# Laying out a pair's queries half a step later, between two value products that share one PSUM buffer

## The chip, the cores and the metric

The kernel runs on one core of a Trainium2 chip. The metric is the device time of one execution in microseconds, the median of several runs. Engines are named as in the profile: PE is TensorE's matmul row and PEld its weight loads, DVE is VectorE, ACT is ScalarE, POOL is GpSimd, SP issues DMAs.

## What is computed

Sliding-window attention with a few sink keys, then a dense MLP over its output, then a mixture of experts. In the reference, cut to what matters:

```python
scores = scale * np.matmul(q, k.transpose(0, 1, 3, 2))       # 4 x 8 heads, 768 x 768, head size 64
keep = is_sink | in_window                                   # 4 sink keys, window of 128
scores = np.where(keep, scores, -1000000000.0)
a = softmax(scores)
x = np.matmul(a, v)                                          # becomes 3072 tokens x 512
h = np.maximum(x @ w_in, 0.0)                                # 512 -> 2048
x = h * h @ w_out                                            # 2048 -> 512
# then: gate logits, one expert of 8 per token, two more products, scaled
```

## The kernel before

The work has three stages: a start in which weights are converted and split into a high and a low part, a first MLP with the attention laid into it (to about 820 us), and the experts. The change concerns the second.

The 3072 tokens are taken in 12 blocks of 256. A pass of the first MLP goes over one block: 16 hidden products (`l1`, L546, twelve matmuls of 256 columns, because each operand is split in two) and 16 output products (`l2`, L562, six matmuls of 512 columns) two steps behind. Each hidden or output product is a half-step, so a pass has 32 of them. `l1`'s result is squared and split on ScalarE and VectorE (L549, L550, L552, L553).

While pass t - 1 runs, the attention of block t is computed, cut into events that carry a time in half-steps. `attn_events` lists them and `run_to` emits those that are due after each half-step. A block has 8 heads in four pairs p of two heads, and two query tiles n of 128 for each pair. The events are:

- `prep_k`: the keys of a pair are transposed on TensorE (L319) and copied and split.
- `prep_q`: the queries of a pair are transposed (L345, two matmuls with the identity) into a PSUM tile `psq`; ScalarE copies the high part (L356), VectorE subtracts for the low part (L357). The values of the pair are split on GpSimd (L363, L364), and `more` issues the loads of the pair after the next.
- `scores`: the score products (L404), mask and maximum on VectorE (L408, L410), exponential on ScalarE (L412), the sum's reciprocal (L414, L415), scaling on ScalarE (L424), and the sink part on GpSimd (L427 to L429).
- `ptrans`: the weights are transposed (L439), copied and split (L450 or L458, L451 or L459), and masked on GpSimd (L455).
- `pv`: the value products (L479) into a PSUM tile `pso`, read by ScalarE (L484 to L486) and VectorE (L487, L488).
- `fin_sink` and `add_sink` at the end of a block: the sink weights are transposed (L496) and multiplied with the sink values (L504) into a PSUM tile `pso2`, read by VectorE (L505).

`psq`, `pso` and `pso2` have the same tag in the pool `psO`, which has one buffer:

```python
psO = ps1.enter_context(tc.tile_pool(name="psO", bufs=1, space=PSUM))
ps = psO.tile([128, 4, 128], F32, tag="O", name="psq")
ps = psO.tile([128, 2, 2, 128], F32, tag="O", name="pso")
```

The times of the events come from the table `LEADS`, with one row for block 0, one for block 1 and one for all later blocks (columns: lead of `prep_k`, lead of `prep_q`, lag of `ptrans`, lag of `pv`):

```python
h0 = 32 * (t - 1) - 8
a0, a1, a2, a3 = LEADS[min(t, 2)]
ev.append((h0 + 8 * p - a1, lambda p=p: prep_q(t, p)))
ev.append((h0 + 4 * n + a3, lambda n=n: pv(t, n // 2, n % 2)))
```

The gate of the block before runs in the same pass, in four pieces (`gate_pieces`): two with four transposes each (L592; ScalarE L601 and L603, VectorE L602, GpSimd L604), the logits (L615, a chain of small VectorE operations and two exponentials on ScalarE, L633 and L634), and the places (L649, L650). They meet pair 2, pair 3, pair 0 and pair 1 in this order, eight half-steps apart. At the end of a pass `split_x` splits the attention's output into the input of the next pass (L512 on ScalarE, L513 on VectorE).

The code is written in the order of these events, and a scheduler then sets the order of each engine's queue from it; each engine executes its queue in that order.

Of the kernel before, what the change touches and what calls it, by code (L numbers as in the profile page):

```python
# [31 lines left out]
T32 = 2  # L32


LEADS = ((5, 2, 4.5, 8.5), (5, 2, 4.5, 8), (5.5, 2.5, 4.5, 8))

SPLITS = {6: (0, 0), 8: (2, 0), 11: (0, 1), 12: (1, 0), 13: (2, 1), 14: (3, 0)}
NSLOT = NT // 128 + NE - 1
# [4 lines left out]
def kern(ctx, tc, q, k, v, n_sink, window, w_in, w_out, w_gate, w_og, w1, w2, out):  # L43
# [471 lines left out]
    def attn_events(t):  # L515

        ev = []
        h0 = 32 * (t - 1) - 8
        a0, a1, a2, a3 = LEADS[min(t, 2)]
        for p in range(4):  # L520
# [578 lines left out]
```

## Time and profile before

| what | value |
|---|---|
| median of 3 runs | 1193.41 us (1192.56 to 1198.88) |
| the profiled execution, its own time | 1196.3 us |
| its span, first to last instruction | 1194.5 us |
| busy in the span: PE, PEld | 1138.7 us (95%), 945.7 us (79%) |
| busy in the span: DVE, ACT, POOL | 761.5, 626.5, 457.9 us |
| L546 (hidden products), matmuls | 314.8 us, 2304 of 285 ns |
| L562 (output products), matmuls | 159.0 + 157.8 us, 1152 of 410 ns |
| L345 (query transposes), matmuls | 21.7 us, 96 of 305 ns |
| mean granted clock of TensorE | 0.991 of full |

The matmul rows overlap one another, since matmuls are pipelined: the distance between two starts says more than the sum of durations. Times below are counted from the span's start.

### The profile page before, as it was taken

The page shows a single profiled execution, that of the slowest core. Times are in us where ns is not written, and L with a number is a line of the kernel's source. Part 1 is how long each engine was busy: PE and PEld are TensorE (multiplying, and loading weights), DVE is VectorE, ACT ScalarE, POOL GpSimd, SP SyncE. Part 2 cuts the span into 40 slices and gives each one's busy share as a digit, 9 for nine tenths or more (in the row PEclk, how much of TensorE's full clock was granted, in tenths as well). Part 3 has the DMA queues.
Part 4 walks back from the last instruction along what each step waited for, and adds up shares of the span by engine and source line. Part 5 has one row for each costly group of instructions (what it writes and reads, how often), then busy time and mean ns, then how long its engine had stood idle before and what let it go on. Part 6 is the DMA issues. An engine that isn't in the chain of part 4 may idle for free. (4 is left out here: it accounts for less than half of the span.)

```text
span 1194.5 us, 24037 instructions
## 1 busy us (share of the span) xinstructions
PE 1138.7 (95%) x7022; PEld 945.7 (79%) x7022; DVE 761.5 (64%) x2123; ACT 626.5 (52%) x1740; POOL 457.9 (38%) x949
## 2 busy tenths in 40 slices
PE   4898889999999999999999999999899999999996
PEld 2476678888888888888888888887788888888884
DVE  4699776767676667676767677656611466764153
ACT  3677576767666766666676666545222222222200
POOL 4256665326565335555424556310211222222111
PEclk9999899999999999999999999999999999999998
DMA  4565411111211211121112120087411357554110
GB/s 123 132 181 176 137 35 45 32 51 37 54 32 28 50 37 46 35 49 29 47 35 51 37 54 1 19 182 207 133 39 44 100 179 255 189 203 151 42 51 23
DMA packets 139387, 100.08 MB, mean 84 GB/s; under 512 B 103903, under 2 KB 112223, under 8 KB 139234
## 3 DMA queue, kind: packets, MB, share of 16 engines
q1 hardware_dynamic: 132674, 83.85, 25.1%
q0 software_dynamic: 5472, 14.19, 3.6%
q8 instruction: 64, 1.05, 0.4%
q14 instruction: 89, 0.73, 0.3%
q10 hardware_dynamic: 1088, 0.26, 0.1%
HBM read 85.56 MB, written 13.76 MB: 83 GB/s over the span
## 5 line engine op out<-in xcount | busy, mean ns | idle before, releaser
L546 PE MATMUL psh<-xT,WI 128*128 128x256 f32 x2304 | 314.8, 285 | 10.6 <-POOL WI L284 8.1
L546 PEld LDWEIGHTS psh<-xT,WI 128*128 128x128 f32 x2304 | 294.9, 190 | 29.0 <-POOL WI L284 10.9
L867 PE MATMUL psh<-WI,xt 128*128 (+1 forms) x672 | 164.8, 400 | 0.3 <-ACT ht L847 0.3
L562 PE MATMUL psx<-WOb,h 128*128 128x512 f32 x576 | 157.8, 410 | 2.7 <-ACT h L552 2.4
L562 PE MATMUL psx<-WOa,h 128*128 128x512 f32 x576 | 159.0, 409 | 0.0
L867 PEld LDWEIGHTS psh<-WI,xt 128*128 128x128 f32 x672 | 124.3, 188 | 27.9 <-ACT xt L847 0.5
L550 DVE TENSOR_TENSOR r<-r 128x256 f32<-128x256 f32 x184 | 83.6, 455 | 68.3 <-ACT r L549 66.7
L562 PEld LDWEIGHTS psx<-WOb,h 128*128 128x128 f32 x576 | 102.6, 191 | 23.4 <-ACT h L552 3.9
L412 ACT ACTIVATE P<-P,st 128x260 f32<-128x260 f32 (+1 forms) x192 | 92.7, 485 | 47.4 <-DVE st L410 45.1
L883 DVE TENSOR_TENSOR ht<-psht,ht 128x512 fp32r<-128x512 f32 x56 | 38.5, 689 | 123.9 <-ACT ht L847 123.5
L549 ACT ACTIVATE r<-psh 128x256 f32<-128x256 f32 x192 | 72.2, 377 | 83.6 <-PE psh L546 72.4
L562 PEld LDWEIGHTS psx<-WOa,h 128*128 128x128 f32 x576 | 102.1, 190 | 17.4 <-issue 0.3
L553 DVE TENSOR_TENSOR h<-r,h 128x256 fp32r<-128x256 f32 x192 | 91.9, 479 | 29.3 <-ACT h L552 25.7
L905 POOL DMA_INDIRECT out_dram<-xg,pidx x28 | 31.2, 1116 | 193.5 <-ACT xg L904 152.0
L408 DVE CUSTOM_DVE_ANT_0 P<-pss,M 128x260 f32<-128x260 f32 (+1 forms) x184 | 72.5, 403 | 28.2 <-PE pss L404 14.3
L455 POOL TENSOR_SCALAR_AFFINE_SELECT PT<-PT 128x256 fp32r<-128x256 f32 x224 | 85.1, 415 | 12.9 <-DVE st L410 12.8
L552 ACT ACTIVATE h<-r 128x256 fp32r<-128x256 f32 x192 | 78.1, 408 | 22.2 <-DVE r L550 18.0
L896 PE MATMUL psy<-WOb,ht 128*128 (+1 forms) x336 | 85.1, 402 | 0.0
L896 PE MATMUL psy<-WOa,ht 128*128 (+1 forms) x336 | 84.1, 397 | 0.0
L873 ACT ACTIVATE r<-psh 128x512 f32<-128x512 f32 x48 | 28.7, 598 | 99.7 <-PE psh L867 97.8
L838 POOL DMA_INDIRECT xg<-x2tab,pidx x30 | 40.7, 1356 | 95.5 <-issue 55.9
L489 POOL TENSOR_TENSOR xr<-tB,tC 128x128 f32<-128x128 f32 x80 | 37.6, 470 | 97.8 <-DVE tB L488 95.3
(430 smaller groups left out, 1979.3 us busy)
## 6 DMA issues: line engine op xcount, KB each, us to landing
raw<-in_moe_w_dram SPq DMA_DIRECT2D x36, 1024.0 KB, 6.2
craw<-in_moe_w_in_dram SPq DMA_DIRECT2D x16, 512.0 KB, 3.8
craw<-in_moe_w_out_dram SPq DMA_DIRECT2D x16, 512.0 KB, 3.2
x2tab<-x2s SPq DMA_DIRECT2D x24, 256.5 KB, 3.1
kn<-in_k_dram SPq DMA_DIRECT2D x64, 96.0 KB, 2.3
vn<-in_v_dram SPq DMA_DIRECT2D x64, 96.0 KB, 2.2
qn<-in_q_dram SPq DMA_DIRECT2D x92, 64.0 KB, 2.1
kn<-in_k_dram SPq DMA_DIRECT2D x32, 64.0 KB, 2.1
```

What stands on the lines that cost most here:

```text
L408: V.tensor_tensor_reduce(out=P[:, e, 0:W], in0=ps[e][:, 0:W], in1=mask[:, 0:W], scale=1.0, scalar=-3.0e38, op0=ALU.add, op1=ALU.max, accum ...
L412: A.activation(out=P[:, e, 0:W], in_=P[:, e, 0:W], func=AF.Exp, scale=SCALE, bias=st[:, 2 + e:3 + e], accum_out=st[:, 4 + e:5 + e])
L455: G.affine_select(out=both[:, 1 - b, e], in_=bf[:, 0, e], pattern=[[0, 2], [1 - 2 * b, 128]], compare_op=ALU.is_gt if b else ALU.is_ge, fi ...
L546: PE.matmul(ps[:], lhsT=WI[:, j, a_, kk, :], rhs=x[:, b_, kk, :], start=(n == 0), stop=(n == 11))
L549: A.activation(out=hq[:], in_=ps[:], func=AF.Relu)
L550: (G if t == 0 and j % 2 else V).tensor_tensor(out=hq[:], in0=hq[:], in1=hq[:], op=ALU.mult)
L552: A.activation(out=o[:, 0], in_=hq[:], func=AF.Copy)
L553: V.tensor_tensor(out=o[:, 1], in0=hq[:], in1=o[:, 0].bitcast(F32), op=ALU.subtract)
L562: PE.matmul(acc[t][m][:], lhsT=o[:, a_, 128 * m:128 * m + 128], rhs=WO[j // 8][:, j % 8, b_, :], start=(j == 0 and n == 0), stop=(j == NF ...
L838: G.indirect_dma_start(out=x, out_offset=None, in_=x2tab[:] if s >= PRE else x2tab[0:256 * (NBLK - 3)], in_offset=bass.IndirectOffsetOnAxi ...
L867: PE.matmul(ps[:], lhsT=o[:, a_, kk, :], rhs=wview(n, par + 2048 * b_ + 512 * kk, 512), start=(c == 0), stop=(c == 11))
L896: PE.matmul(yp[s][:], lhsT=o[:, a_, kk, :], rhs=wview(2 + n, par + 2048 * b_ + 512 * kk, 512), start=(n == 0 and kk == 0 and c == 0), stop ...
```

## The change

For the blocks from 2 on, `prep_q` has a lead of 1.5 half-steps where it had 2.5. The value products of the pair before are at 0 and 4 half-steps (of eight), so the layout was emitted after half-step 5 and is now emitted after half-step 6, halfway to the next value product. Ten blocks with four pairs each are touched, 40 of the 48 layouts. No instruction is added or taken away.

```diff
-LEADS = ((5, 2, 4.5, 8.5), (5, 2, 4.5, 8), (5.5, 2.5, 4.5, 8))
+LEADS = ((5, 2, 4.5, 8.5), (5, 2, 4.5, 8), (5.5, 1.5, 4.5, 8))
```

What this does to the queues shows at three places. In the names, `psx` is the output products' accumulator, `psh` a hidden product, `psg` the gate's tile, `pss` scores, `h` the split hidden values.

TensorE, a pair that meets the gate's transposes, before:

```order
L439 MATMUL pspt<-ident,P 128x128 x2
L562 MATMUL psx_7034<-WOa,h_7114 128x512 x3
L562 MATMUL psx_7035<-WOa,h_7114 128x512 x3
L345 MATMUL psq<-ident,qn 128x128 x2
L546 MATMUL psh<-xT,WI 128x256 x12
L592 MATMUL psg<-ident,x2s 128x128 x4
L562 MATMUL psx_7034<-WOa,h_7185 128x512 x3
L562 MATMUL psx_7035<-WOa,h_7185 128x512 x3
L546 MATMUL psh<-xT,WI 128x256 x12
L479 MATMUL pso<-PT,V 128x256 x4
```

Here the query transposes stand right behind the output products, ahead of the hidden one. With the change:

```order
L439 MATMUL pspt<-ident,P 128x128 x2
L562 MATMUL psx_7034<-WOa,h_7114 128x512 x3
L562 MATMUL psx_7035<-WOa,h_7114 128x512 x3
L546 MATMUL psh<-xT,WI 128x256 x12
L592 MATMUL psg<-ident,x2s 128x128 x4
L345 MATMUL psq<-ident,qn 128x128 x2
L562 MATMUL psx_7034<-WOa,h_7185 128x512 x3
L562 MATMUL psx_7035<-WOa,h_7185 128x512 x3
L546 MATMUL psh<-xT,WI 128x256 x12
L479 MATMUL pso<-PT,V 128x256 x4
```

The query transposes moved behind one hidden product and the gate's four transposes; one output and one hidden product remain between them and the value products.

ScalarE at the same place, before:

```order
L450 ACTIVATE PT<-pspt 128x2x128
L356 ACTIVATE qT<-psq 128x256
L412 ACTIVATE P,st<-P,st 128x260 x2
L549 ACTIVATE r<-psh 128x256
L601 ACTIVATE x2T<-psg 128x512
L424 ACTIVATE P<-P,st 128x132 x2
L552 ACTIVATE h_7310<-r 128x256
L603 ACTIVATE x2T<-x2U 128x512
L549 ACTIVATE r<-psh 128x256
L484 ACTIVATE tB<-pso 128x256
```

Here L356 stands ahead of the two exponentials (L412). With the change:

```order
L450 ACTIVATE PT<-pspt 128x2x128
L412 ACTIVATE P,st<-P,st 128x260 x2
L549 ACTIVATE r<-psh 128x256
L601 ACTIVATE x2T<-psg 128x512
L424 ACTIVATE P<-P,st 128x132 x2
L552 ACTIVATE h_7290<-r 128x256
L603 ACTIVATE x2T<-x2U 128x512
L356 ACTIVATE qT<-psq 128x256
L549 ACTIVATE r<-psh 128x256
```

The copy of the query tile (L356) moved from ahead of the exponentials to behind L603, the second copy of the gate's transposes.

TensorE at the end of a pass, a pass in which the sink values are added, before (the query transposes stand ahead of these rows, two groups earlier):

```order
L504 MATMUL pso_7832<-pskT,vsk 128x256 x2
L562 MATMUL psx_7034<-WOb,h_7689 128x512 x3
L562 MATMUL psx_7035<-WOb,h_7689 128x512 x3
L562 MATMUL psx_7034<-WOb,h_7727 128x512
L509 COMPARE_AND_BRANCH
L509 UNCONDITIONAL_BRANCH x2
L562 MATMUL psx_7034<-WOb,h_7727 128x512 x2
L562 MATMUL psx_7035<-WOb,h_7727 128x512 x3
L479 MATMUL pso<-PT,V 128x256 x4
L404 MATMUL pss_7871<-kT,qT 128x260
```

Here the sink products (L504) come after the query tile has been read, and the value products come straight behind the output products. With the change:

```order
L504 MATMUL pso_7812<-pskT,vsk 128x256 x2
L562 MATMUL psx_7034<-WOb,h_7689 128x512 x3
L562 MATMUL psx_7035<-WOb,h_7689 128x512 x3
L562 MATMUL psx_7034<-WOb,h_7727 128x512 x2
L509 COMPARE_AND_BRANCH
L509 UNCONDITIONAL_BRANCH x2
L345 MATMUL psq<-ident,qn 128x128 x2
L562 MATMUL psx_7034<-WOb,h_7727 128x512
L562 MATMUL psx_7035<-WOb,h_7727 128x512 x3
L404 MATMUL pss_7871<-kT,qT 128x260
L404 MATMUL pss_7872<-kT,qT 128x260
L404 MATMUL pss_7871<-kT,qT 128x260
```

The query transposes now stand behind the sink products, with eight output products between. The value products follow the last row, so three of the six score products stand ahead of them.

## Rows read from the trace of the kernel before

**Rows 1.** Busy time by stretches: us; busy PE, PEld, DVE, ACT, POOL; clock, DMA, GB/s.

```profile
350.00:430.00 80.00, 78.45 (x559) 68.04 (x559) 54.56 (x195) 54.53 (x170) 36.70 (x90) 1.00 0.15 35
```

**Rows 2.** Groups by line, the whole run: busy us, mean ns | idle before, releasers.

```profile
L345 PE MATMUL psq<-ident,qn 128*128 128x128 f32 x96 | 21.7, 305 | 6.6 <-ACT PT L450 2.7 <-issue 0.9 <-DVE qT L352 0.5
...
L345 PEld LDWEIGHTS psq<-ident,qn 128*128 128x128 f32 x96 | 10.8, 148 | 23.7 <-issue 18.3 <-ACT PT L450 4.5 <-DVE qT L352 0.8
```

**Rows 3.** Waits of PE from 200 to 1000 us: us in total, times, longest.

```profile
PE psq L345 <- ACT PT L450: 2.7, 3, 1.0
...
PE psst L496 <- POOL psk L429: 1.1, 3, 0.5
```

**Rows 4.** Timeline of PE, a pair at the gate's transposes: start us, duration us.

```profile
364.59 0.64 PE L479 MATMUL pso<-PT,V 128*128 128x256 f32 x4
...
365.92 1.64 PE L562 MATMUL psx<-WOa,h 128*128 128x512 f32 x6
...
367.69 0.41 PE L345 MATMUL psq<-ident,qn 128*128 128x128 f32 x2
...
367.85 1.65 PE L546 MATMUL psh<-xT,WI 128*128 128x256 f32 x12
...
369.34 0.60 PE L592 MATMUL psg<-ident,x2s 128*128 128x128 f32 x4
...
369.69 1.64 PE L562 MATMUL psx<-WOa,h 128*128 128x512 f32 x6
...
371.17 1.57 PE L546 MATMUL psh<-xT,WI 128*128 128x256 f32 x12
...
372.58 0.64 PE L479 MATMUL pso<-PT,V 128*128 128x256 f32 x4
```

**Rows 5.** Timeline of ACT and DVE in the same stretch.

```profile
367.18 0.29 DVE L488 TENSOR_TENSOR tB<-pso,tB 64x128 f32<-64x128 f32 x1
...
368.13 0.38 ACT L356 ACTIVATE qT<-psq 128x256 fp32r<-128x256 f32 x1 [1.12 <-PE psq L345]
...
368.20 0.16 DVE L410 TENSOR_SCALAR st<-st 128x2 f32<-128x2 f32 x1
...
368.42 0.50 ACT L412 ACTIVATE P<-P,st 128x260 f32<-128x260 f32 x1
...
368.55 0.42 DVE L357 TENSOR_TENSOR qT<-psq,qT 128x256 fp32r<-128x256 f32 x1 [0.20 <-ACT qT L356]
...
368.91 0.50 ACT L412 ACTIVATE P<-P,st 128x260 f32<-128x260 f32 x1
...
369.60 0.38 ACT L549 ACTIVATE r<-psh 128x256 f32<-128x256 f32 x1
...
369.98 0.60 ACT L601 ACTIVATE x2T<-psg 128x512 bf16<-128x512 f32 x1
...
370.18 0.40 DVE L550 TENSOR_TENSOR r<-r 128x256 f32<-128x256 f32 x1
...
370.47 0.69 ACT L424 ACTIVATE P<-P,st 128x132 f32<-128x132 f32 x2
...
370.61 0.69 DVE L602 TENSOR_TENSOR x2U<-psg,x2T 128x512 f32<-128x512 f32 x1
...
371.06 0.41 ACT L552 ACTIVATE h<-r 128x256 fp32r<-128x256 f32 x1
...
371.37 0.62 ACT L603 ACTIVATE x2T<-x2U 128x512 bf16<-128x512 f32 x1
...
371.50 0.42 DVE L553 TENSOR_TENSOR h<-r,h 128x256 fp32r<-128x256 f32 x1 [0.20 <-ACT h L552]
```

**Rows 6.** Timeline at the end of a pass, PE and DVE.

```profile
338.12 0.48 PE L504 MATMUL pso<-pskT,vsk 128*128 128x256 f32 x2
...
339.50 0.68 DVE L505 TENSOR_TENSOR xr<-pso,xr 128x512 f32<-128x512 f32 x1
...
341.24 0.63 PE L479 MATMUL pso<-PT,V 128*128 128x256 f32 x4
```

## The prediction

> **What bounds the kernel now.** I read the busy time by stretches first. In the steady part of the first MLP, with the attention spread through it, TensorE is busy for 78.45 of 80 us at full clock and no other engine is busy for more than 55 [rows 1]. So a change of order gains only what TensorE waits, and it loses whatever new wait it creates on TensorE. Next come the groups by line. The query transposes (L345) are preceded by 6.6 us of idle time on the matmul row over the whole run, and by 23.7 us on the weight-load row [rows 2]. The list of waits then gives the two waits that matter below. Three query transposes waited 2.7 us in all, put down to ScalarE's copy of PT, and three sink transposes waited 1.1 us for GpSimd [rows 3].
>
> The page doesn't name the real releaser, so I went to the timeline. The query transposes and the value products share one PSUM buffer (tag O, one copy). The transposes can start only when VectorE's last read of the earlier value product (L488) is done. L488 ends at 367.18 + 0.29 = 367.47 [rows 5], and the transposes start at 367.69 [rows 4]: 0.22 us from the end of a VectorE read to the start of the matmul that waited for it. In the same rows the output products (L562) start at 365.92 and the transposes 1.77 later. The next six output products, with nothing that waits behind them, need 1.48 (369.69 to 371.17). **The wait is thus 1.77 - 1.48 = 0.29 us in this pair.**
>
> **The removed wait.** Forty query layouts move (ten half-blocks of four pairs). At the new place, after the next hidden product (L546) and its gate work, L488 has long ended: the transposes would start at 365.92 + 1.48 + 1.49 + 0.35 = 369.24. (1.49 is L546 to L592 and 0.35 is L592 to L562 [rows 4].) That is 1.77 us after 367.47. Nothing is added to any engine: the same instructions, the same loads. The loads that `more` issues come 2 to 3 us later and are used two pairs later, each pair about 15 us (two value products apart by 7.99 here), so SP's queue hides them. The 40 waits are worth 40 x 0.29 = 11.6 us. The three long ones [rows 3] can add 2.7, and the matmul row's own idle time, 6.6, is the lower bound. If nothing else happened the gain would be 6.6 to 14.3 us; I take 10.
>
> What the weight-load row shows is larger, 23.7 us [rows 2]. The Trainium skill (Perfetto Trace Analysis, Identifying the Most-Contended Engine) says that matmul busy share is a bad measure of headroom and that the busy share of weight loads is the one to read. By that rule all 23.7 us would be headroom; by the spacing of matmul starts, half of it was covered by running products.
>
> **The new wait, at the transposes of the gate.** The buffer is also needed by the next value product, which must now wait until both readers of the query tile (ScalarE L356, then VectorE L357) have finished. Before, they had two products' and the gate's time, and L357 ended at 368.55 + 0.42 = 368.97, 3.61 us ahead of the value product at 372.58 [rows 4, 5]. Now the order on ScalarE decides. L356 stands behind both scalings of P (L424), L552 and L603. The steps, in the clock of the timeline [rows 4, 5]:
>
> - TensorE, if nothing waited: transposes 369.24, output products 0.16 later (367.69 to 367.85) at 369.40, L546 at 370.88, value product 1.41 later (371.17 to 372.58) at 372.29. That is 0.29 ahead of before.
> - ScalarE: the second L412 starts at 368.91 as before, since the first waits for L410, not for TensorE. L549 can follow after 0.49 (the distance of the two L412) at 369.40, 0.20 earlier than before. L601 and L424 gain the same.
> - L603 does not gain. It needs L602, and L602 stands behind L550 (370.18 + 0.43 = 370.61, the old start). L602 ends at 370.61 + 0.69 = 371.30, and L603 stays at 371.37.
> - L356 starts about 0.51 after L603 (L601, as long as L603 within 0.02, is followed after 0.49): 371.88. L357 starts 0.42 later (368.13 to 368.55) at 372.30 and ends at 372.72; its engine is free by then, as L553 ends at 371.92. With 0.22 to TensorE the value product starts at 372.94.
>
> So the value product comes at 372.94 instead of 372.58: **0.36 us later**, where the clean order would have brought it 0.29 earlier. I take 0.35. Bounds: below, 0.15, if ScalarE runs its queue closer than these distances; above, 0.55, if the weights behind the wait cost their 0.1 as well and the score products stand behind it. Nineteen of the twenty transposes of the gate that meet a moved layout have L603 ahead of L356. In the first one L356 comes first, and that one gains 0.29. Sum: 19 x 0.35 - 0.3 = **+6.4 us**. In the three pairs with the long wait VectorE's whole chain is late and L603 with it, so the same 0.35 applies there.
>
> **At the end of a pass** (pair 1, ten layouts) the moved transposes stand behind the sink product of the heads (L504), which uses the same buffer and is read by L505. In one such pair L504 starts at 338.12 [rows 6]. Moved up by the 0.45 of wait and transposes, followed after 0.32 (338.12 to its successor) by eight output products at 0.247 (1.48 / 6), the transposes are reached at 339.97. L505 ends at 339.50 + 0.68 = 340.18, so with 0.22 they wait until 340.40, some 0.4. Then L357 stands behind two pieces of the split (L513), and the value product, 341.24 before [rows 6], comes near 342.0 with half the score products ahead of it: net +0.5 us. Three passes have this order. The other seven have L505 earlier or no sink product: between -0.29 and +0.5, and I take 0. Sum **+1.5**, bounds -0.5 to +5.
>
> **At the logits** (pair 0, ten layouts) L356 comes right behind L552, with 1.48 + 1.41 of products as cover. In most of them TensorE reaches the sink transposes earlier and waits there for GpSimd's L429 [rows 3], whose chain did not move. Between -0.29 and 0; I take -0.1 each, **-1.0**.
>
> Sum 6.4 + 1.5 - 1.0 = **+6.9 us**. Against the profiled execution (1196.3 us, 2.9 above the median of the runs shown) that is 1203.2; against the median, 1193.4 + 6.9 = **1200.3 us**.
>
> **Rivals.**
>
> 1. *The clean gain* (faster). The wait goes and none follows, because ScalarE reaches L356 in time. It needs the value product's buffer free by 372.29, so L356 at 371.23, 0.65 ahead of my time. Against it: L603 alone starts at 371.37 and stands ahead in an in-order queue. Time 1193.4 - 10 = 1183.4. That all 23.7 us come back (1169.7) is possible only if the weight loads were the limit.
> 2. *The freed ScalarE* (no change). L356 no longer stands in front of L412, where ScalarE sat idle for 1.12 us [rows 5], so the whole chain starts earlier. For it: L412 started 0.29 after L356 did. Against it: L410 ends at 368.36, 0.06 before L412 starts. If it moves the chain by 0.29, the value product comes at 372.65, +0.07 each: 19 x 0.07 + 1.5 - 1.0 = 1.8, 1195.2 us.
> 3. *The pass end becomes the bound* (much slower). L513 behind L357 delays the split input, and the first hidden product of each pass waits a further 1 us: ten passes, 1200.3 + 10 = 1210.3. Against it: the last two pieces are needed only six products into that group.
>
> **How the numbers follow.** Forecast 0.65, its own range 1194.5 to 1205 (19 x 0.15 to 19 x 0.55, with part of the pass-end bounds). Freed ScalarE 0.20. Clean gain 0.09, and all of the weight-load idle 0.01. Pass end 0.05. A measurement can tell about 0.5%, 6 us, from no change: 1187.4 and 1199.4. The forecast lies above 1199.4 in two thirds of its cases (0.44), and with the pass end slower has 0.49; faster has 0.10; the same has 0.41. The range that leaves out the clean gain, the pass end and the tails is 1190.5 to 1205.
>
> **What would show it.** The transposes start without idle time before them, and their row of waits is gone. New waits of TensorE appear at L479 (and L404), put down to qT L357 or L356, 0.4 to 0.7 us each, some twenty of them. The distance of the two value products around a gate transpose is about 8.3 us instead of 7.99. It is wrong if L479 doesn't wait, or if L603 ends far earlier against the value product before it.

## The result, and the profile after

| | median | runs | profiled execution | its span |
|---|---|---|---|---|
| before | 1193.5 us | 6 (1191.53 to 1198.88) | 1196.3 us | 1194.5 us |
| changed | 1202.9 us | 6 (1200.11 to 1204.08) | 1200.11 us | 1198.3 us |

The ratio is 1.0071, with a 95% interval of 1.0047 to 1.0094: the change makes the kernel slower, by 0.7%. Two repeats gave 1.0061 (1.0040 to 1.0083) and 1.0065 (1.0043 to 1.0086). Ratios leave out two executions far above the rest, one of e3 (1383.6 us) and one of e5 (2749.4 us). By the numbers the forecast (1200.3 us, slower) held. **By its steps it held only in part: the attention gives about 2 us of the loss, and 4.6 us come from a place that the prediction did not look at.**

The page of the changed kernel: its first line, and the busy times.

```profile
span 1198.3 us, 23987 instructions
...
PE 1138.9 (95%) x7022; PEld 951.3 (79%) x7022; DVE 755.4 (63%) x2123; ACT 621.9 (52%) x1740; POOL 450.5 (38%) x949
```

TensorE is as busy as before; the span is longer by idle time. The instruction count is 50 lower (24037 before): the same computation, but not the same instructions, since some of the small ones that carry waits are gone. Counted in the trace with those of its sequencer, TensorE has 15649 instructions instead of 15703, VectorE 8 more and ScalarE 4 fewer. That will matter.

The groups by line, for the two lines that share the buffer (busy, mean ns of one | idle time before, and what ended it):

```profile
L479 PE MATMUL pso<-PT,V 128*128 128x256 f32 x296 | 50.7, 291 | 4.9 <-DVE qT L357 4.9
...
L345 PE MATMUL psq<-ident,qn 128*128 128x128 f32 x96 | 21.7, 305 | 1.2 <-DVE qT L352 0.5 <-DVE xr L505 0.4
...
L345 PEld LDWEIGHTS psq<-ident,qn 128*128 128x128 f32 x96 | 11.8, 150 | 6.3 <-DVE xr L505 3.5 <-issue 2.0 <-DVE qT L352 0.8
```

The idle time before the query transposes fell from 6.6 to 1.2 us on the matmul row and from 23.7 to 6.3 on the weight-load row [rows 2]. In its place 4.9 us stand before the value products, all put down to L357. The list of waits of TensorE, 200 to 1000 us, says the same (total, times, longest):

```profile
PE psxt L853 <- DMA xg<-x2tab,pidx: 5.7, 1, 5.7
PE pso L479 <- DVE qT L357: 4.2, 12, 0.4
PE psst L496 <- POOL psk L429: 2.9, 6, 0.7
```

The 2.7 us of long waits at L345 [rows 3] are gone and the wait for L357 is there. The sink transposes (L496) wait longer than the 1.1 us of [rows 3], as forecast at the logits. But the first row is new in size too. It is the gather of the first expert tokens after the last gate, one wait of 5.7 us; the two profiles of the kernel before have 3.3 and 2.7 there. I return to it.

The pair of [rows 4, 5] on TensorE, ScalarE and VectorE of the changed kernel:

```profile
364.38 0.64 PE L479 MATMUL pso<-PT,V 128*128 128x256 f32 x4
...
368.59 0.60 PE L592 MATMUL psg<-ident,x2s 128*128 128x128 f32 x4
369.02 0.38 PE L345 MATMUL psq<-ident,qn 128*128 128x128 f32 x2
369.16 1.64 PE L562 MATMUL psx<-WOa,h 128*128 128x512 f32 x6
370.64 1.57 PE L546 MATMUL psh<-xT,WI 128*128 128x256 f32 x12
372.54 0.71 PE L479 MATMUL pso<-PT,V 128*128 128x256 f32 x4 [0.33 <-DVE qT L357]
```

```profile
370.14 0.70 ACT L424 ACTIVATE P<-P,st 128x132 f32<-128x132 f32 x2
370.75 0.40 ACT L552 ACTIVATE h<-r 128x256 fp32r<-128x256 f32 x1
371.05 0.61 ACT L603 ACTIVATE x2T<-x2U 128x512 bf16<-128x512 f32 x1
371.57 0.36 ACT L356 ACTIVATE qT<-psq 128x256 fp32r<-128x256 f32 x1
```

```profile
370.29 0.68 DVE L602 TENSOR_TENSOR x2U<-psg,x2T 128x512 f32<-128x512 f32 x1
...
371.97 0.42 DVE L357 TENSOR_TENSOR qT<-psq,qT 128x256 fp32r<-128x256 f32 x1 [0.36 <-ACT qT L356]
```

The chain L602, L603, L356, L357, L479 is the predicted one, link by link, and the value product waits 0.33 us for it. From value product to value product it is 372.54 - 364.38 = 8.16 us, against 7.99 before and 8.35 predicted.

### The profile page after: what moved, and what is told of

The parts are those of the page before. It is cut to its first block, busy times and chain, and to the rows that moved or that the text cites. A ratio compares the mean times of both kernels' runs of the same rounds, so it can differ in the third digit from the quotient of the medians.

```text
span 1198.3 us, 23987 instructions
## 1 busy us (share of the span) xinstructions
PE 1138.9 (95%) x7022; PEld 951.3 (79%) x7022; DVE 755.4 (63%) x2123; ACT 621.9 (52%) x1740; POOL 450.5 (38%) x949
## 5 line engine op out<-in xcount | busy, mean ns | idle before, releaser
L546 PEld LDWEIGHTS psh<-xT,WI 128*128 128x128 f32 x2304 | 298.6, 190 | 32.4 <-POOL WI L284 11.7
L546 PE MATMUL psh<-xT,WI 128*128 128x256 f32 x2304 | 312.0, 284 | 11.0 <-POOL WI L284 8.9
L412 ACT ACTIVATE P<-P,st 128x260 f32<-128x260 f32 (+1 forms) x192 | 93.2, 486 | 93.6 <-DVE st L410 93.0
L550 DVE TENSOR_TENSOR r<-r 128x256 f32<-128x256 f32 x184 | 82.7, 450 | 51.2 <-ACT r L549 50.5
L549 ACT ACTIVATE r<-psh 128x256 f32<-128x256 f32 x192 | 71.4, 373 | 75.6 <-PE psh L546 67.0
L455 POOL TENSOR_SCALAR_AFFINE_SELECT PT<-PT 128x256 fp32r<-128x256 f32 x224 | 87.6, 426 | 14.4 <-DVE st L410 13.0
L896 PEld LDWEIGHTS psy<-WOa,ht 128*128 128x128 f32 x336 | 62.7, 188 | 14.7
```

Of the source, the lines that this page charges most:

```text
L412: A.activation(out=P[:, e, 0:W], in_=P[:, e, 0:W], func=AF.Exp, scale=SCALE, bias=st[:, 2 + e:3 + e], accum_out=st[:, 4 + e:5 + e])
L455: G.affine_select(out=both[:, 1 - b, e], in_=bf[:, 0, e], pattern=[[0, 2], [1 - 2 * b, 128]], compare_op=ALU.is_gt if b else ALU.is_ge, fi ...
L546: PE.matmul(ps[:], lhsT=WI[:, j, a_, kk, :], rhs=x[:, b_, kk, :], start=(n == 0), stop=(n == 11))
L549: A.activation(out=hq[:], in_=ps[:], func=AF.Relu)
L550: (G if t == 0 and j % 2 else V).tensor_tensor(out=hq[:], in0=hq[:], in1=hq[:], op=ALU.mult)
L896: PE.matmul(yp[s][:], lhsT=o[:, a_, kk, :], rhs=wview(2 + n, par + 2048 * b_ + 512 * kk, 512), start=(n == 0 and kk == 0 and c == 0), stop ...
```

## Where the time went

All profiles of this study divide at the same four instructions: the first gate logits (L615) of a pass in the first and in the tenth pass that has them, the first transposes of the expert stage (L853), and the end of the last matmul. These two rows of each profile, start of the first logits and of the tenth, give the second column; first of e8, a second profile of the kernel before, then of e9, a second one of the changed kernel:

```profile
197.97 0.23 PE L615 MATMUL psg<-w,x2T 128*128 128x80 bf16 x2
...
757.21 0.23 PE L615 MATMUL psg<-w,x2T 128*128 128x80 bf16 x2
```

```profile
198.58 0.23 PE L615 MATMUL psg<-w,x2T 128*128 128x80 bf16 x2
...
759.38 0.23 PE L615 MATMUL psg<-w,x2T 128*128 128x80 bf16 x2
```

| profile | to first logits | 1st to 10th logits | to first L853 | L853 to the end |
|---|---|---|---|---|
| before | 197.79 | 559.42 | 65.39 | 360.36 |
| before, again (e8) | 197.97 | 559.24 | 64.51 | 359.86 |
| changed | 196.15 | 561.55 | 64.45 | 364.63 |
| changed, again (e9) | 198.58 | 560.80 | 64.58 | 364.49 |
| changed, again (e10) | 196.77 | 560.76 | 65.12 | 364.60 |
| e1: pairs 2, 3 late | 194.62 | 562.76 | 64.50 | 360.31 |
| e2: pairs 0, 1 late | 197.79 | 557.81 | 64.50 | 361.42 |
| e3: changed, 2 and 3 ahead | 198.00 | 562.52 | 65.55 | 360.02 |
| e4: all at 2.05 | 194.92 | 560.69 | 64.52 | 361.58 |
| e6: pairs 0, 1 at 2.05 | 197.78 | 556.52 | 65.58 | 361.57 |
| e7: pair 1 late | 200.24 | 559.70 | 64.46 | 361.72 |
| e11: changed + transposes | 205.66 | 561.54 | 64.55 | 359.70 |
| e12: before + transposes | 207.68 | 559.63 | 64.68 | 359.90 |

The second column repeats within 0.2 us for the kernel before and within 0.8 for the changed one. The first moves by some us from run to run, with the changed kernel alone from 196.15 to 198.58. Between the two repeats (e9 less e8) the columns differ by +0.61, +1.56, +0.07 and +4.63; together 6.87, and the spans (1199.9 and 1193.1) by 6.8.

## The experiments

In all runs the blocks from the third on are edited, in the place where the event of a query is made: the lead becomes one number per pair.

```diff
-ev.append((h0 + 8 * p - a1, lambda p=p: prep_q(t, p)))
+ev.append((h0 + 8 * p - (a1 if t < 2 else QL[p]), lambda p=p: prep_q(t, p)))
```

**e1, only the pairs at the gate's transposes:** `QL = (2.5, 2.5, 1.5, 1.5)`.

> Only the queries of pairs 2 and 3 of each block (the two ahead of the gate's transposes) move to the later place; pairs 0 and 1 stay at the earlier one. Theory A (the loss comes from these pairs, because the queries' copy L356 then stands behind the gate's L601 and L603 on ScalarE and the second value product waits for it): the distance between the two value products of such a pair goes from 7.99 to about 8.15 us, the profile shows some twelve to twenty waits of L479 on qT L357, and the time is 3 to 9 us over the kernel before (ratio 1.0025 to 1.0075). Theory B (the loss comes from pairs 0 and 1: pass end and logits): the time is that of the kernel before within 2 us. Theory C (the loss lies outside the attention passes, in the start or in the expert stage, by the placing of their transfers): no difference between this one and the next one that follows the pairs.

Measured: 1198.0 us against 1194.7 for the kernel before, ratio 1.0027 (1.0005 to 1.0049). Its line L479 shows the wait alone:

```profile
L479 PE MATMUL pso<-PT,V 128*128 128x256 f32 x296 | 50.0, 287 | 6.2 <-DVE qT L357 6.2
```

The distance in these pairs is 8.17 to 8.24 instead of 7.99 to 8.06, and 8.00 to 8.03 instead of 7.80 to 7.85 in every third block, which has the shorter ones; the three long pairs named below (8.72 to 8.80) are at 8.90 to 9.18. The passes are 3.3 us longer. Theory A holds for these pairs.

**e2, only pairs 0 and 1:** `QL = (1.5, 1.5, 2.5, 2.5)`. (The expectations of e1 and e2 name the two the wrong way round: pair 0 stands at the logits, pair 1 at the pass end.)

> The counterpart: only pairs 0 (pass end) and 1 (gate logits) move to the later place. Theory A: within 2 us of the kernel before (ratio 0.998 to 1.002), no wait of L479 on qT L357 at the gate's transposes, whose distance stays 7.99. Theory B: 4 to 10 us over the kernel before, nearly the whole loss, with the pass-end distances at 8.1 to 8.5 against 7.8 to 7.95. Theory C: as the run above.

Measured: 1194.9 us against 1194.7, ratio 0.9987 (0.9971 to 1.0003): no difference shown, and theory B falls. The passes are 1.5 us shorter. e1 and e2 add to 1.8 us in the passes, which is what the changed kernel has there; of its 6 to 9 us in all that explains little.

**e3, pairs 2 and 3 just ahead of the gate's pieces:** the changed kernel with `QL = (1.5, 1.5, 2.05, 2.05)`.

> The changed kernel, but the queries of pairs 2 and 3 have a lead of 2.05 in place of 1.5: they fall due in the same half-step, just ahead of the gate's transposes, so that L356 stands ahead of L601 and L603 on ScalarE and the psq transposes ahead of the gate's on TensorE; pairs 0 and 1 as in the changed kernel. Theory A: the waits of L479 on L357 go, the pair's distance comes to 7.7 to 8.0 us, and the time is 5 to 12 us under the changed kernel, at 1191 to 1198. A rival within A (the gate's pieces, now later, are what is late): the waits move to the gate's L601/L603 chain or to psq's own wait for L488, and the time stays within 3 us of the changed kernel's. Theory B: the time stays at the changed kernel's 1203, since pairs 0 and 1 are as there.

Measured: 1199.49 us against 1194.7, ratio 1.0037 (1.0020 to 1.0054). The wait for L357 is gone and the distance is 7.65 to 7.69 us, 0.15 to 0.4 under that of before (the last pair, 8.49, apart). Yet the passes take 562.52, longer than the changed kernel's (560.8 to 561.6), because the stretch behind each such pair became some 0.5 us longer (seventeen of them 134.1 us in place of 125.4 in e8). By the passes the rival within A won, though the wait moved to a place that it did not name. The total lies 3.4 us under the changed kernel's, since the expert stage takes 360.02 here. The list of waits of TensorE, one row per layout of keys:

```profile
PE psk__4288 L319 <- DVE PT L451: 0.5, 1, 0.5
```

Seventeen such rows (0.2 to 0.8 us) for L319 are on it, none before. On VectorE of this run:

```profile
495.31 0.41 DVE L357 TENSOR_TENSOR qT<-psq,qT 128x256 fp32r<-128x256 f32 x1
...
496.69 0.69 DVE L602 TENSOR_TENSOR x2U<-psg,x2T 128x512 f32<-128x512 f32 x1
498.35 1.21 DVE L550 TENSOR_TENSOR r<-r 128x256 f32<-128x256 f32 x1 [0.97 <-ACT r L549]
...
501.38 0.42 DVE L451 TENSOR_TENSOR PT<-pspt,PT 128x256 fp32r<-128x256 f32 x1
```

The queries passed the gate, so the gate's L602 and L603 are late, behind them L549 and L550, and at the end of the chain L451, for whose buffer the next keys wait. In these pairs the order on ScalarE decides who is late, not whether.

**e4, all pairs at 2.05.**

> All queries with a lead of 2.05: after the half-step that the change leaves behind, but ahead of whatever else falls due in the same half-step (gate pieces, the sink product at the pass end). Theory A: like the run above at the gate's transposes; where the pass end and the logits also lost, another 1 to 3 us are saved: 1188 to 1197. Rival (any place nearer to the first value product makes psq wait for its eviction L488): waits of PE at L345 of 0.1 to 0.3 us in 30 or more pairs, and 1196 to 1206.

Measured: 1197.51 us, ratio 1.0015 (0.9996 to 1.0033): no difference shown, and theory A's 1188 to 1197 is missed. The rival falls: the idle time before L345 is 0.5 us in all. The passes are 1.4 us longer than before, with the same waits of the keys as in e3.

**e5, the changed kernel again.**

> The changed kernel once more, unaltered, for a second profile and more runs. The passes from the first to the tenth gate logits were 2.1 us longer in its first profile than in that of the kernel before (561.55 against 559.42), and moving pairs 2 and 3 alone (+3.2 us of the median) and pairs 0 and 1 alone (-1.5 us, no difference shown) add to +1.7; the first runs said +9.4. Theory A (the change costs what the passes show, the rest of the first difference was the granted clock outside the passes): 1.5 to 5 us over the kernel before (ratio 1.001 to 1.004), passes again 561 to 562, and a clock without the dip to 0.98 between 822 and 1000 us. Theory C (the change costs more than its passes show, in the start or the expert stage): 7 to 11 us again (ratio over 1.006), with the passes at 561 to 562 and the surplus at the same place as in the first profile, after the first expert tiles.

Measured: 1203.71 us against 1196.07, ratio 1.0061 (1.0040 to 1.0083): theory C's number. The profiled execution spans 2747.6 us. In it a matmul of L546 took 531 ns in the mean instead of 285, at a granted clock of 1.00 by the profile, so it tells nothing of the place.

**e6, pairs 0 and 1 at 2.05:** `QL = (2.05, 2.05, 2.5, 2.5)`.

> Pairs 0 and 1 at 2.05, pairs 2 and 3 at the 2.5 of the kernel before. By the pass lengths of the four runs before this (each stretch from logits to logits taken from the run in which its pairs stood so): about 61.7, 61.25 and 62.5 in turn, 556.5 to 557.5 from the first to the tenth logits, 2 to 3 us under the kernel before: 1191 to 1193, ratio 0.9975 to 0.9985. Rival (the stretches are not independent: what one place gains another takes up): passes at 558.5 to 560, no difference to the kernel before.

Measured: 1193.0 us against 1196.07, ratio 0.9972 (0.9955 to 0.9989), passes 556.52 us. The three stretches of the expectation, three times each, add to 556.35, so it is met to 0.2 us: from logits to logits the stretches add up. This version beats both kernels, the one before by 0.3%.

**e7, pair 1 alone:** `QL = (2.5, 1.5, 2.5, 2.5)`.

> Only pair 1, the pass end, moves to the later place. (In the expectations of the first two runs the names are the wrong way round: pair 0 is followed by the gate's logits, pair 1 by the pass end.) Expected from the distances in the changed kernel: +0.52 at three pass ends, +0.34 at three, -0.38 at three to four: about +1 us in the passes, 560 to 561, and the time within 2 us of the kernel before. Rival (the pass end alone carries the gain of the run with pairs 0 and 1): passes 557.5 to 558.5.

Measured: 1197.24 us, ratio 1.0014 (0.9995 to 1.0034); passes 559.70. The pass ends stand at +0.5, +0.35 and -0.38 (8.47, 8.10 and 7.32 against 7.95, 7.75 and 7.70), nine together +1.4. The passes are under the 560 to 561 expected, because the three gate pairs with the long wait (two in e8) went from 8.72 to 8.80 us to 8.05, here and in e2 and e6, and not in e1: their lateness came from the early queries of the pass end before them.

**e8, the kernel before again.**

> The kernel before, unaltered, for a second profile: passes 559 to 560 from the first to the tenth logits, if that length is steady; start and expert stage to be compared with the first profile's (197.8 us to the first logits; 360.4 us from the first expert transposes to the end), to see by how much they move of themselves. Theory A: they move by 2 us or more with the granted clock. Theory C: they stand within 1 us.

Measured: 1194.75 us against 1196.07, ratio 0.9989 (0.9970 to 1.0007). Start and expert stage stand within 0.2 and 0.5 us of the first profile's, as theory C had it.

**e9 and e10, the changed kernel twice more.**

> The changed kernel again, unaltered, since the profile of the repeat before this fell into an execution with TensorE at half speed throughout (2747.6 us) and shows nothing, while its six other executions gave 6 to 9 us over the kernel before, as the first ones had; the passes, 2.1 us longer in the one sound profile, hold only a part of that. Theory C1 (start): the first gate logits come at 200 us or later, against 197.8 and 198.0 in the two profiles of the kernel before (196.15 in the first profile of the changed one, at a lower mean clock), by a dip of the granted clock between 100 and 200 us that the moved layouts of the first passes bring on; passes 561 to 562. Theory C2 (expert stage): from the first transposes of the experts to the end 364 us or more again (359.9 and 360.4 in the kernel before), with the wait for the gather at 5 us or more and a dip of the clock behind it. Theory P (passes): the passes are 564 us or longer in a usual execution. The total should again be 6 to 9 us over the kernel before.

> As the run before it: a third profile of the changed kernel, to tell what is steady in it (passes, by all theories but P at 561 to 562) from what moves with the execution (start and expert stage).

Measured: e9 1201.85 us against 1194.08, ratio 1.0065 (1.0043 to 1.0086); e10, a single run, 1200.59. Theory C2: the expert stage takes 364.5 us in all three profiles, and the wait for the gather is 5.3 to 5.7. C1 falls, as the first logits come at 198.58 and 196.77, and P falls. In the stretch of 10 us in which TensorE waits (length, busy of the five engines, granted clock, DMA), e9 and then e8:

```profile
850.00:860.00 10.00, 4.64 (x17) 3.55 (x17) 2.65 (x4) 0.60 (x1) 2.97 (x3) 0.75 0.39 88
```

```profile
850.00:860.00 10.00, 7.73 (x36) 6.33 (x37) 4.12 (x3) 1.89 (x3) 3.31 (x4) 1.00 0.66 194
```

The wait is 2.7 us longer, and with it the granted clock drops: its mean in this stretch is 0.75 of full (0.66 and 0.70 in the other two), so part of it was at 1.2 GHz; in e8 it stayed at 2.4. From 850 to 870 us the mean is 0.83 in all three. Why is the gather late? It needs the row places (`pidx`), six small loads on SP's queue behind the last scatter. What the trace gives for that tile, e9 and then e8 (minimum, median and maximum ns of the issue; first and last start):

```profile
L834 SPq DMA_DIRECT2D pidx<-perm x6: 333/333/2553, 848.4 to 856.0; - x6
```

```profile
L834 SPq DMA_DIRECT2D pidx<-perm x7: 43/333/343, 845.7 to 861.1; - x7
```

One issue takes 2553 ns in place of 333 (2021 and 2407 in the other two profiles). It is the second in e9; the row on SP's queue, and the only other transfer that the DMA view shows from 848.5 to 849:

```profile
849.48 2.55 SPq L834 DMA_DIRECT2D pidx<-perm  x1
```

```profile
q8 instruction: 1, 0.02, 36.8%
```

That is one packet of 16 KB of instructions, and its share is 0.368 x 16 engines x 0.5 us = 2.9 us of one DMA engine: it starts at 848.70 and ends at 851.65, and the slow issue ends at 852.03, 0.38 later. In the other two profiles the slow issue ends 0.40 and 0.39 us after the packet.

That an issue on SP's queue is held until such a packet has ended is no matter of the changed kernel alone. In the first profile of the kernel before, two loads of keys:

```profile
532.53 4.83 SPq L306 DMA_DIRECT2D kn<-in_k_dram  x2
```

The second starts at 532.95, takes 4.41 us and ends 0.40 after a q8 packet. In all thirteen usable profiles 96 issues on SP's queue after 220 us took over 1 us. Of these, 83 overlap a q8 packet and end 0.2 to 0.8 us behind it (nearly all 0.3 to 0.5); the rest are one load of expert weights (L805) in eleven profiles, and one L834 in each of e11 and e12. But not every load is held: 20 other L834 that began while a q8 packet was under way were issued in 0.34 to 0.57 us.

The same packet, the 45th on q8, in every profile:

| profile | TensorE's instructions | packet after the start of the last scatter L658 | slowest L834 behind it |
|---|---|---|---|
| changed (three) | 15649 | 8.2 us | 2.0 to 2.6 us |
| e1 | 15669 | 5.0 | 0.35 or less, here and below |
| e3 | 15671 | 4.8 | |
| e2 | 15683 | 3.3 | |
| e7 | 15684 | 3.0 | |
| e4 | 15695 | 1.9 | |
| before, e8 | 15703 | 1.1 | |
| e6 | 15707 | 0.4 | |

The fewer instructions TensorE has, the later the packet comes, and the loads begin 7.4 to 8.1 us after the scatter. Only the changed kernel has it among them. The packet carries TensorE's program: in all thirteen profiles it comes when TensorE has started 11088 to 11111 instructions, whether 11027 (changed), 11081 (before) or 11113 (e12) of them lie ahead of the scatter; and the 64 packets of q8 come some 250 TensorE instructions apart in every stage. (The expectation of e11 has the packet up to 0.5 us earlier and goes by the instructions of all engines; the times here are the packet's own start.)

**e11 and e12, the packet shifted:** 14 transposes at the start, their result unused; with them TensorE has 28 instructions more in e11 (15677) and 32 more in e12 (15735).

```diff
-make_identity(nc, ident)
+make_identity(nc, ident); pad = psT.tile([128, 4, 128], F32, tag="T", name="pad"); [PE.transpose(pad[:, n % 4], ident[:], ident[:]) for n in range(14)]
```

> The changed kernel with 14 extra transposes of the identity on TensorE at the very start, ahead of its first wait for data (their result is not read); nothing else is edited, though the scheduler shifts some instructions of the first layouts. In the three sound profiles of the changed kernel one of the six loads of row places L834 takes 2.0 to 2.6 us to issue in place of 0.34, and each time a 16 KB load of the instruction queue q8 falls among them, 7.8 to 8.0 us after the last scatter L658; in the eight other profiles it falls 0.0 to 4.5 us after it, earlier the more instructions the profile counts (23987 here, 24037 in the kernel before), and every L834 takes 0.35 us or less. Theory I (TensorE's own program, shorter by some waits since the change, is fetched at another place, and the fetch collides with these loads): 28 more instructions bring the fetch to 1 to 4 us after the scatter, every L834 takes under 0.4 us, TensorE's wait for the gather L853 falls from 5.4 to about 3, and from the first L853 to the end it takes 360 to 362 us in place of 364.5. Theory S (the slow issue is the change's in another way, by SP's own queue): L834 and the 364.5 stay as they are. The passes are 561 to 562 by both.

> The control: the kernel before with the same 14 transposes at the start. Theory I: the fetch moves to some 5 us ahead of the scatter's end, where it meets none of these loads; passes 559 to 560 and the expert stage 360 to 361.7 as without them, so that the changed kernel with the transposes stands 1 to 4 us over this one (6 to 9 without them). Theory S: the difference stays at 6 to 9 us.

Measured, e11: the packet comes 4.2 us after the scatter, and the same two rows now read

```profile
PE psxt L853 <- DMA xg<-x2tab,pidx: 2.7, 1, 2.7
```

```profile
L834 SPq DMA_DIRECT2D pidx<-perm x6: 167/333/343, 855.7 to 861.2; - x6
```

From L853 to the end it takes 359.70 us instead of 364.5, with the passes at 561.54 as in the changed kernel. Theory I holds and S falls. The control meets none of the loads, as expected (passes 559.63, expert stage 359.90), though its packet comes 0.3 us ahead of the scatter's start and not 5 ahead of its end. The totals can't be used: the transposes and the shifted start cost 7 to 10 us up to the first logits in both (1204.27 and 1207.11 us against 1194.4), more in the control. So the comparison of totals that e12's expectation names was not to be had. From the first logits to the last matmul e11 takes 1.6 us more than e12 (985.79 and 984.21); without the transposes it was 6.3 (989.87 in e9, 983.61 in e8).

## Why the prediction was right, and where it was wrong

- **The removed wait.** Right in place: the wait of L345 for L450 left the list, and 1.2 us of idle time are left on its matmul row. At the gate this brought no gain, as predicted.
- **The weight-load row.** Its idle time fell by 17.4 us and the passes grew longer, so that idle time was no headroom. The Trainium skill (Perfetto Trace Analysis, Identifying the Most-Contended Engine) judges TensorE's headroom by the busy share of all weight loads, beside the share of peak; that share stood at 79% before and after. To read the idle time of one row by it, as the prediction's second reading did, was a step beyond the page.
- **The new wait at the gate (+6.4).** Right in mechanism, wrong in size; this is the step of the passes that failed. Against a distance of 7.99 it cost 0.16 us (0.20 in the third kind of block) in place of 0.35. Two inputs were off. The chain before L603 ran 0.1 us earlier than I let it, part of what the rival of the freed ScalarE supposed: moved to this profile's start of 364.38, the prediction has L602 at 370.40, and it came at 370.29. And from the end of L357 (372.39) to the matmul it took 0.15, not the 0.22 seen at L345. "The same 0.35 applies" in the three long pairs was wrong: they became 0.5 us shorter (8.72 to 8.22), since their lateness came from a place that the change also moved. That the first pair "gains 0.29" was wrong too: L356 does stand ahead of L603 there, but ScalarE had sat idle for 1.47 us until L410, L479 still waited 0.35 us for L357, and the pair is 0.41 longer (8.48 in e9, 8.07 in e8). From the first to the tenth logits lie eighteen of the twenty pairs: in e9 less e8 fifteen at about 0.17, two long ones at -0.5 and the last unchanged, +1.5. All twenty give +2.1 in place of +6.4.
- **Pass end (+1.5).** Right: +0.52 at each of the three pass ends where +0.5 was forecast. Where 0 was forecast it was +0.35 and -0.38, three times each; nine together +1.4.
- **Logits (-1.0).** The sum is right: nine distances add to 78.70 us in e9 and 80.05 in e8, -1.4 (-0.6 between the first two profiles). It isn't -0.1 each: the three passes without sink transposes have 0.35 less (8.89 to 8.54), and most of the others hardly moved, as the wait at the sink transposes would have it.
- **The sum in the passes** is thus about +1.5; the column says +1.6. From 163 us to the first logits, where the two other gate pairs stand, another 0.36 is lost. These 1.9 us alone would have given about 1195.4, "the same" by the prediction's own 6 us, and near the figure of the rival of the freed ScalarE (1195.2), though not by its +0.07 a pair.
- **What was missing: +4.6 in the expert stage.** I counted "nothing is added to any engine" and stopped there. TensorE's program became shorter by 54 instructions, it was fetched at other times, and one fetch met the row-place loads. The loss of 6.8 us came near the forecast of 6.9 by this accident: the number was right by luck. The Trainium skill (Runtime: NRT & Kernel Launch, Instruction fetch mechanics) describes a fetch in blocks of 16 KiB on a DMA queue of its own and calls its cost mostly hidden. The packet size agrees. TensorE shows no wait in the 2.9 us of the packet itself; the cost fell on SP's queue, and came back to TensorE through the gather.

Left open: by what way the packet holds the issue of a 0.5 KB load on another queue until it has landed, why other loads that begin during a packet are not held, and why most packets near the scatter last 2.7 to 3.9 us where others last about 1. Of the 0.61 us in the first column 0.36 is the two gate pairs named above; the rest is less than the start moves from run to run.

## What to carry to other kernels

When a wait for a shared buffer is moved, follow the buffer to its next writer: the wait moves there, and its size is set by who stands ahead of the readers in their queues. When the total differs from the sum of the stretches, divide both profiles at the same instructions before explaining anything. And where a short chain of small loads gates a stage, look at what else the DMA queues carry then, the instruction queue included: a change of order moves that too.

## What was unexpected in the hardware

- A 0.5 KB load took 2.0 to 2.6 us to issue instead of 0.33 when a 16 KB packet of TensorE's instructions was under way, in three profiles of three, and ended 0.4 us behind it; these six loads were not slow in the ten others. The same hold, up to 4.4 us, stands in every profile at other loads, the kernel before included, where no wait of TensorE for these loads is on the list.
- That delay cost more than itself. In e9 less e8 it is 2.7 us of waiting; the other 1.9 of the expert stage's 4.6 go with the granted clock, 0.83 from 850 to 870 us in the three profiles. In the profiles with the usual wait of 2.7 to 3.3 us the stage took 359.7 to 360.4 where the clock stayed at 1.00 there, and 361.4 to 361.7 where it was 0.91.
- A matmul that waited for VectorE started 0.15 us after it at L479 and 0.22 us after it at L345.
